# A fused attention and two-layer mixer on one core: another written order for the jobs of its first part

## The chip, the cores and the metric

The kernel runs on one core of a Trainium2 chip. The core has five engines that run side by side, each through its own list of instructions in order: TensorE (PE, matrix products; its weight loads are shown as PEld), VectorE (DVE), ScalarE (ACT), GpSimd (POOL) and SyncE (SP), which here only issues DMA transfers. An engine waits at an instruction until the semaphores it needs are set; everything behind that instruction waits too. The metric is the device time of one execution in microseconds (us), the median of several runs.

## What is computed

Everything is float32 outside; B = 2, H = 8, S = 768, D = 64.

```python
k_sum = k.reshape(B, H, 24, 32, D).max(axis=3)
v_sum = v.reshape(B, H, 24, 32, D).mean(axis=3)
scores_l = where(|t - s| < 16, q @ k.T / 8, -1e9)
scores_s = q @ k_sum.T / 8 + log(32)
a = softmax(concat([scores_l, scores_s]))
x = a @ concat([v, v_sum])                    # heads side by side: B x 768 x 512
h = relu(x @ w_in); u, v = halves(h)
v_s = w_spatial @ layernorm(v) + b_spatial
y = (u * v_s) @ w_out
h2 = relu(y @ w_in2); c = conv3(h2, conv_w)   # along the sequence
out = (h2 * sigmoid(c)) @ w_out2
```

## The kernel before

**Attention** runs over eight pairs of heads (n = 0 to 7), each in two groups of six 64-row blocks, so 16 groups. One group is a chain over four engines: PE writes masks and scores into PSUM (`qk`, L496, L503, L509), DVE takes the row maximum (L513), ACT does six exponentials with their sums (L517), DVE adds and inverts the sums (L520, L523), POOL or DVE normalises (L526), PE transposes the first half (L530), ACT or DVE copies it out of the one PSUM tile `pt` (L552), PE transposes the second half into the same `pt`, a second copy follows, PE multiplies with the values (`pv`, L536), and ACT or DVE splits the result into a high part (L557) and a low part (L558). There are two score buffers `s` and four buffers of exponentials, so several groups are under way at once. Beside that, `keys` prepares windows of k (L424, L422, L438) and block maxima (L432); `means` prepares the block means of v, for two pairs by products on PE (L452), for the others by a DVE sum (L459) and one transposition (L462), followed by a copy (L464) and spreads (L469, L471).

**Dense products** are done in three passes on high and low parts (`mm3`, L344 to L346). The first layer's weights come as raw 64-bit words and are rebuilt by `convert` (L307 or L308, L310, L312, L314, L298, L292). PE does the first layer's products (`f1u`, `f1v`) between the groups of attention, and only dense products after about 97 us. Later come the spatial mix by a seven-product scheme, the merged weights `w_out @ w_in2`, the convolution with its gate, and the last layer, again with seven products.

**What sets the order.** Every job (some instructions that belong together) is entered with `Plan.add`, with the engines that can do it and what it reads and writes. `Plan.order` then takes two tables of the file: `ORDER`, the numbers of all 1579 jobs, two characters each, in the order in which they are written out, and `PICK`, which of two or three engines does a job that can go to several. Each engine's list is its jobs in that order. `Plan.order` also adds up durations written in the file (the first number of each entry), and where PE would stand still for 0.5 us or more by these, it writes dummy products in front of the job (`warm`, L1085):

```python
gap = t - free.get(e, 0.0)
if self.fill and gap >= 0.5:
    n = int((gap - 0.1) / 0.22)
```

So the dummies depend on the order and on the file's own durations, and the table carries none of them. SP issues the loads in the order in which their jobs stand. A load into a buffer that is used again waits for the last reader of what lay there.

Of the kernel before, what the change touches and what calls it, by code (L numbers as in the profile page):

```python
# [54 lines left out]
ORDER = (
    "AAACABADAFAgAEAiAGAjAZAaAkAhAbAHAqAcAdAeArALBYAfAMBZBbBaBcAIA3A4AsAJAlAtASAUATAVAWAuAvANBiBjAKBEA5A6A7BFCTCRCUBkAmAnAwAx"
    "AOBvAyAzA8B8CVDJCSBGBwB9DKCbAoApBlBmBnAXDLA9A0A+CcA-BADHDIBxBHBoBRCoBSA1A2BBCdByBzB0BpBqCpBCAYCeAPBdCfCgBDB+DRBrB1B2C1Be"
    "BfBgBhDSEgCqCrCsB3DwEhB-AQCDDeDfB4CEBsChBICWCtBtBuCiDTBKBLEeBJBMBTBNBOCFDgCXCYCjARB5BUCZB6BVCGCHCICJB7C2CAEnETDUDVEoDrCk"
    "CuClCmCnEfCKC3CvCwCaDhDMBPDWBQFNE0DiCxEpCyCzDXC0DYEqErDsCBDxDNDODPBWDjFMDZDaDAC5DtDQFOFPDkDlC6DbDcE1E2DmDnCCDyEUFVDdDoEs"
    "EtDpEuC7C8C9C+C-BXEiDqDBCLFiEvFjE3E4EjEkDzD0EwFvCMCNDuDvCOCPD6DCDDDED7D8D9D1D+D2EEEFD3FBCQEGE5EmDFDGFkEHEIE6D4F6F7EOEPEQ"  # L60
    "ERGmD5F8F9C4FCD-EAEBECFWEXE7FFFGEYEZEaEbGnFHFIFJFKElFXEDE8GlEcEdE9FYFLGkFZFlFaGQGRGDE+ExEJEKELESHPGSGEGFEyFmE-FAFnEzFbFz"
    "F0EMFwGtG6GdEVJwFQFRFcFdF1ENHHHIGeF2F3GfGGGgF4FeHQFSFTF5FoHJFUHRGhGiGjFpFqFrGuFDG7HSHTHKHLEWFsG8GTGUGHF+GVGIFtHMHNFuFfFg"
    "HiHjFxHkHlGJFyG9G+HOHUHXHYGvGKGwHZHVFhHmHWIhGLGMF-GxGyGAHyGBHnIDHzHaGWGXImGCH0FEGoH1HbHcGYHoHqGNGZGaGbHrHsGOGcGPHdG-JtGz"
    "JuIrItIuHtIcG0H2HeGpG1HuIdIiHfIwH3GqG2IsM-INGrJxIOJzGsHvJ3HAIPHBIIHgH4HCInHDG3NBHwG4HEG5IjIvHFIXJ6IJHhJ0IEIYIKNAJ4HGNCIQ"
    "JvIeH5IZJ1IaIbIRIkIFJ5IfIxJyIyIzJBHxJCISJDHpIgILH8I0H+KbJ2H6KBJ8IlITNNKCJEH9H-IMI5H7NDKFI6IBI1I7KDIUIAIoI8JRKcJFKGI9J7NG"
    "NJJGICKHIVKXJ9JHNII2I+I3JSIWJTJUKAKYI-JJJVJIJZJaI4J-JbNEJAJcIpJKKIJWJhKEJLJdJMNFKJNHIqLDJiJeNKLHJXNUJNKQJfIGJjJ+KKJOIHKd"
    "KhJYKRJPJgLIJQKiJmKLLJJoKjNQKSJkKeNLJnLEJpJlJrLFKfKzKlKsKmKtJsKuK0KnKgKZKaLLKMLMK9KTNPLKNMK5LGKkK7LPNOLNK-K+LTNbNRKNLQNS"
    "K6NTNWLXLRLBKvLUNXLOK8LYLZLbKONVNYLVLSNiLcLdNZLALfLgLWNdLeLaKoNeLhLiNaLlLzNcKPNfLCLoL2NpLjKpNgLmNhLpNkL3NlNjLnLkL0L4MOMB"
    "NmJqKqMPMcNnKUMHL1NrNoMQNsNwKrLrNqMINtK1MEMJMRL5MCNuKVMVMdMFNzNvLqNyPXMWKWN3PLMXMDNxK3L6KwL7N0MYN1MeMmPYMnN5K4MfPMMsN2N6"
    "MGK2N4N7LvN+PZPNPaKxN8MoKyN9OAOBMKL9MzMtLsLwN-OCPbMjMuOFPOODPdOHM0PROILxPPMLMkPSOEM7OGOJMpLtPvMqPTMlMrOMPeL+OKPfPQMvOOOL"  # L70
    "OPONOTM3L-MwMxP1P2PpM4OQOUPjMMPkPUPcOaOROWMyLyOVOSMSPlOhPqM5MgM8PVPgP3PWM1MAPmMhOcM9PrOdObM6P7LuP4MZM2MiP8PnQFOXOeM+MaP5"
    "PhPsOkMbQAQGQBPwMNOjL8QCOfOiPiMTMUOoQHQDTXQIP9OYOqOrOpTYOlPtOsQJP+OgPxTdQEP-OmOvPoOtO2PyTeOuPuQXOyP6QYOxQKQcQLQdQMOwOzQZ"
    "O4QaO9O5QeO3PzQbQSQTOnQUQfO6QNQOO-OZQgQVRFO0RAPEQWQPQhPAO7PGO+QuPFP0QQQzO8O1RKQiQjQ0Q1QpTZQvPBQqQRPHQrQsQ2PIQkQwTaQxTjTf"
    "RBRLQlQtRGRcQ3TgQyRCQmQ4TpTrRDRMRHRXRIRNRYQ5TlRZU-RhRiQ6TsQnPCRdThRER2QoTbRJRsRxTiTqRORtRPTcUwRaTkTmT2UxRQQ7RjRyReQ8TtRR"
    "RfTuRzRkR3T3UrPJRTQ9RuPKR4RSR0TnRbQ+RgRlRvR5U1RmSGSLSMT6ToQ-SBRUSfSCR1RwR6PDTvTwR7SDU2SERnSHRVRoRqRpSFU6R8SIR9R+R-UySNSJ"
# [1155 lines left out]
```

## Time and profile before

| | us |
|---|---|
| median of 3 runs | 321.06 (320.39 to 321.64) |
| the profiled execution, its time | 320.22 |
| its span, first to last instruction | 318.5 |
| PE busy in the span | 310.9 |
| DVE, ACT, POOL busy | 268.8, 236.8, 117.7 |

The profiled execution took 1.7 us more than its span, and 0.84 us less than the median of the runs. Busy time on PE has modelled ends: matrix products overlap, and the end of the last one before a wait covers some of that wait. Idle time is therefore read from the starts of two jobs that follow each other, compared with the same pair where nothing is waited for.

### The profile page before, as it was taken

Reading aid. Unit: us, or ns where it says so; the run is one execution under the profiler, and the core shown is the slowest. Engines: PE = TensorE matmul, PEld = TensorE weight load, DVE = VectorE, ACT = ScalarE, POOL = GpSimd, SP = SyncE. Lnnn points to the kernel's source line nnn. Section 1 sums busy time; section 2 is a strip of 40 time slices with the busy share of each in tenths; the row PEclk is TensorE's granted clock in tenths of the full one; section 3 lists DMA queues with packets and bytes.
Section 4 is the critical chain, followed back from the end, with each engine's and each line's share of the span. In section 5 each row is a group of like instructions: output and inputs, shape, how many; then the busy total and the mean of one; then the engine's idle time right before and its main releaser. Section 6 shows DMA issues by size and latency. Waiting matters only on the chain.

```text
span 318.5 us, 6374 instructions
## 1 busy us (share of the span) xinstructions
PE 310.9 (98%) x2376; PEld 271.6 (85%) x2376; DVE 268.8 (84%) x493; ACT 236.8 (74%) x565; POOL 117.7 (37%) x130
## 2 busy tenths in 40 slices
PE   7999999999999999999999999999999999999994
PEld 3677788888888888999998888888888899999994
DVE  5989899886578978988987787899999999989971
ACT  3999888977385735677987687998788997684721
POOL 3696853814335347254532353100110222254010
PEclk9999999999999999999999999999999999999999
DMA  7999675936453001114433334400110412154432
GB/s 215 333 284 313 180 229 197 314 81 167 160 189 134 1 2 21 45 48 141 135 110 119 114 132 132 132 2 0 25 24 3 75 25 52 25 99 105 129 139 99
DMA packets 16061, 37.64 MB, mean 118 GB/s; under 512 B 1952, under 2 KB 8480, under 8 KB 16032
## 3 DMA queue, kind: packets, MB, share of 16 engines
q1 hardware_dynamic: 13728, 34.11, 33.8%
q0 software_dynamic: 2304, 3.15, 5.8%
q8 instruction: 18, 0.29, 0.4%
q14 instruction: 11, 0.09, 0.1%
HBM read 30.96 MB, written 3.15 MB: 107 GB/s over the span
## 4 chain that ended last, share of the span: by engine, by line
PE 88%; DVE 4%; ACT 3%; POOL 2%; DMA 1%; issue 1%; SPq 0%; DVEq 0%; POOLq 0%
PE late L345 11%; PE late L346 11%; PE late L344 11%; PE mm L344 10%; PE mm L346 9%; PE mm L345 9%; PE pt L530 3%; PE xp L344 3%; PE xp L345 3%; PE xp L346 3%; PE xp L536 3%; PE pt L346 3%; PE pt L344 3%; PE pt L345 3%; PE s L509 2%; DMA a<-q_in 1%
## 5 line engine op out<-in xcount | busy, mean ns | idle before, releaser
L517 ACT ACTIVATE a<-s,a 128x120 f32<-128x120 f32 x96 | 33.3, 381 | 0.9 <-DVE a L513 0.9
L345 PE MATMUL late<-xl,a 128*128 128x512 f32 (+1 forms) x80 | 29.5, 369 | 0.0
L344 PE MATMUL late<-xh,a 128*128 128x512 f32 (+1 forms) x80 | 29.4, 367 | 0.0
L346 PE MATMUL late<-xh,a 128*128 128x512 f32 (+1 forms) x80 | 29.4, 367 | 0.0
L914 DVE SCALAR_TENSOR_TENSOR w<-v,conv_t,w 128x1534 f32<-128x1534 f32 x12 | 21.8, 1818 | 4.1 <-POOL w L908 2.1
L876 POOL DMA_DIRECT2D tmp<-w x9 | 8.4, 932 | 44.3 <-ACT tmp L875 33.0
L517 ACT ACTIVATION_READ_ACCUMULATOR a<-s,a 128x1 f32 x96 | 21.9, 228 | 0.0
L526 POOL TENSOR_TENSOR a<-a,a 128x720 f32<-128x720 f32 x14 | 19.3, 1391 | 5.6 <-DVE a L523 5.5
L292 POOL TENSOR_TENSOR w<-a,w 128x256 fp32r<-128x256 f32 (+2 forms) x13 | 14.2, 1097 | 15.1 <-PE late L345 7.9
L530 PE MATMUL pt<-ident,a 128*120 128x128 f32 x96 | 16.5, 281 | 0.8 <-DVE a L552 0.6
L345 PEld LDWEIGHTS late<-xl,a 128*128 128x128 f32 x80 | 15.0, 188 | 2.4 <-DVE xl L292 0.4
L344 PEld LDWEIGHTS late<-xh,a 128*128 128x128 f32 x80 | 15.0, 188 | 1.9
L346 PEld LDWEIGHTS late<-xh,a 128*128 128x128 f32 x80 | 15.0, 188 | 1.9
L298 ACT CAST w<-a 128x512 fp32r<-128x512 f32 (+2 forms) x17 | 10.0, 589 | 8.4 <-DVE a L314 3.5
L327 ACT ACTIVATE a<-a 128x512 uint16<-128x512 uint8 x20 | 15.7, 787 | 0.0
L330 ACT ACTIVATE a<-a 128x512 f16<-128x512 f32 x20 | 15.6, 782 | 0.0
L530 PEld LDWEIGHTS pt<-ident,a 128*120 128x120 f32 x96 | 10.8, 136 | 5.0 <-POOL a L526 1.0
L513 DVE TENSOR_REDUCE a<-s 128x6 f32<-128x720 f32 x16 | 14.2, 899 | 0.9 <-PE s L509 0.8
L298 ACT CAST xh<-tmp 128x384 fp32r<-128x384 f32 x24 | 12.1, 511 | 3.8 <-DVE tmp L878 2.0
L344 PE MATMUL mm<-w,xh 128*128 128x512 f32 x36 | 14.9, 414 | 0.0
L344 PE MATMUL mm<-xh,a 128*128 128x512 f32 (+1 forms) x40 | 14.7, 367 | 0.0
L346 PE MATMUL mm<-xh,a 128*128 128x512 f32 (+1 forms) x40 | 14.7, 367 | 0.0
(399 smaller groups left out, 1131.7 us busy)
## 6 DMA issues: line engine op xcount, KB each, us to landing
a<-w_in SPq DMA_DIRECT2D x12, 512.0 KB, 3.6
...
```

The costliest lines, as they stand in the source:

```text
L292: eng.tensor_tensor(out=lo.r(), in0=src.f(), in1=hi.f(), op=ALU.subtract)
L298: us = {"ACT": (0.2 + n / 1200, lambda: ACT.copy(hi.r(), src.f())), "POOL": (0.12 + n / 1050, lambda: POOL.tensor_copy(hi.r(), src.f()))}
L327: ACT.activation(out=c.ap.bitcast(U16).rearrange("p (n w) -> p n w", w=2)[:, :, 0], in_=byte, func=AF.Copy, scale=1.0 / 32.0, bias=-15.5 / ...
L330: ACT.mul(c.ap.bitcast(F16).rearrange("p (n w) -> p n w", w=2)[:, :, 1], word(), 2.0 ** -60)
L344: PE.matmul(ps, lhsT=lh, rhs=rh, start=first and i == 0, stop=False, **kinds)
L345: PE.matmul(ps, lhsT=lh, rhs=rl, start=False, stop=False, **kinds)
L346: PE.matmul(ps, lhsT=ll, rhs=rh, start=False, stop=last and i == n - 1, **kinds)
L513: DVE.tensor_reduce(out=st[:, 0], in_=sv, op=ALU.max, axis=AX.X, negate=True)
L517: ACT.activation(out=e[:, u, :NK], in_=sv[:, u // GA, u % GA], func=AF.Exp, bias=st[:, 0, u:u + 1], accum_out=sm[:, u, :1])
L526: eng.tensor_tensor(out=e, in0=e, in1=st[:, 1].unsqueeze(2).to_broadcast([128, GB, NK]), op=ALU.mult)
L530: PE.transpose(pt3[:NK, a], e[:, GA * h + a, :NK], ident)
L914: DVE.scalar_tensor_tensor(out=two(ct)[:, bs, to], in0=two(h)[:, bs, of], scalar=scale(k), in1=two(ct)[:, bs, to], op0=ALU.mult, op1=ALU.add)
```

## The change

Only the two tables differ. Seventeen of the rows of `ORDER` are new; the first 998 of the 1579 places hold the same job numbers in another order, the last 581 are as they were. In `PICK` the first two rows are new, so some jobs change their engine: two normalisations go from POOL to DVE (POOL 14 to 12, DVE 2 to 4); three copies out of `pt`, four casts L557 and one L424 from DVE to ACT; three spreads L469 and two copies L464 from ACT to DVE, one spread L471 from POOL to DVE; one multiplication of `convert` from ACT (L307) to POOL (L308) and, later, three of the second conversion from ACT (L332) to POOL (L333); three subtractions L292 from POOL to DVE. The order of the load jobs among themselves is the same. The dummy products follow from the order: 22 become 27, 17 instead of 13 ahead of the first scores and 10 instead of 9 after them.

```diff
 ORDER = (
-    "AAACABADAFAgAEAiAGAjAZAaAkAhAbAHAqAcAdAeArALBYAfAMBZBbBaBcAIA3A4AsAJAlAtASAUATAVAWAuAvANBiBjAKBEA5A6A7BFCTCRCUBkAmAnAwAx"
+    "ACAFAGAZAgABAjAHAEAiAkAAALAMADAbAIAaAcAdAJASBZANBaAhAqAKA3ArAeAsBYAlBbBcBEATA4AUAtAVAuBiA5AWBFAOB8BjCTBGAvCRAmCUCSCVA6Bk"
...
 PICK = (
-    "001101210000101011001110100010000010100011000100011010100010111010000100010001010101001100011111011000011000100000000001"
+    "111001101100100010110100101001201100100101101000010101000000010000001200010000000110001110010011010100011001100000110001"
```

The first place is PE's list around the fourth group's transpositions, at 22 to 26 us before. `s` are scores, `a_0_100` the exponentials of the fourth group, `pt` and `xp` PSUM tiles, L462 the transposition of the v sums, `mm` the first dense product (`xh`, `xl` times `w`). Before:

```order
L509 MATMUL s_80<-a_0_95,a_0_252 64x120 x12
L530 MATMUL pt<-ident,a_0_100 120x128 x3
L462 MATMUL xp<-ident,a_0_86 24x128
L530 MATMUL pt<-ident,a_0_100 120x128 x3
L344 MATMUL mm_84<-xh_0_93,w_0_192 128x256
L345 MATMUL mm_84<-xl_0_94,w_0_192 128x256
L346 MATMUL mm_84<-xh_0_93,w_0_192 128x256
```

In the changed kernel, the same engine from the same scores on, up to the first of the two transpositions:

```order
L509 MATMUL s_80<-a_0_95,a_0_172 64x120 x12
L462 MATMUL xp<-ident,a_0_86 24x128
L344 MATMUL mm_84<-xh_0_93,w_0_232 128x256
L345 MATMUL mm_84<-xl_0_94,w_0_232 128x256
L346 MATMUL mm_84<-xh_0_93,w_0_232 128x256
L530 MATMUL pt<-ident,a_0_100 120x128 x3
```

and, after the next group's scores, the end of these scores and what follows them:

```order
L509 MATMUL s_81<-a_0_95,a_0_172 64x120 x12
L536 MATMUL xp<-a_0_92,a_0_497 64x64 x12
L530 MATMUL pt<-ident,a_0_100 120x128 x3
L452 MATMUL mm_85<-a_0_168,a_0_86 24x128 x6
```

Before, only L462 stood between the two transpositions of a group into the one tile `pt`; now a whole set of scores and a `pv` stand there, and the dense product comes ahead of both.

The second place is POOL's list from 6 to 17 us, with the first normalisations (L526; `a_0_91` and `a_0_96` are the exponentials of the first two groups). Before:

```order
L308 TENSOR_SCALAR a_0_156<-a_0_156 128x256
L424 TENSOR_SCALAR a_0_95<-a_0_96 128x6x96
L292 TENSOR_TENSOR w_0_192<-a_0_156,w_0_192 128x256
L424 TENSOR_SCALAR a_0_95<-a_0_96 128x6x96
L438 TENSOR_SCALAR a_0_95<-a_0_95 128x12x24
L526 TENSOR_TENSOR a_0_91<-a_0_91,a_0_90 128x720
L526 TENSOR_TENSOR a_0_96<-a_0_96,a_0_95 128x720
L438 TENSOR_SCALAR a_0_90<-a_0_90 128x12x24
L424 TENSOR_SCALAR a_0_90<-a_0_91 128x6x96
L471 TENSOR_SCALAR a_0_236<-a_0_97 24x768 x2
```

In the changed kernel, POOL in the same stretch, up to the third normalisation:

```order
L424 TENSOR_SCALAR a_0_90<-a_0_91 128x6x96
L424 TENSOR_SCALAR a_0_95<-a_0_96 128x6x96
L438 TENSOR_SCALAR a_0_95<-a_0_95 128x12x24
L308 TENSOR_SCALAR a_0_123<-a_0_123 128x256
L526 TENSOR_TENSOR a_0_91<-a_0_91,a_0_90 128x720
L424 TENSOR_SCALAR a_0_90<-a_0_91 128x6x96 x2
L438 TENSOR_SCALAR a_0_90<-a_0_90 128x12x24
L526 TENSOR_TENSOR a_0_96<-a_0_96,a_0_95 128x720
L471 TENSOR_SCALAR a_0_168<-a_0_97 24x768
L526 TENSOR_TENSOR a_0_97<-a_0_97,a_0_90 128x720
```

The preparation of the next pair's keys has moved between the first two normalisations, and the second spread L471 has left POOL ahead of the third.

## Rows read from the trace of the kernel before

**Rows 1.** The page: the span, and PE's busy time and instructions.
```profile
span 318.5 us, 6374 instructions
PE 310.9 (98%) x2376; PEld 271.6 (85%) x2376; DVE 268.8 (84%) x493; ACT 236.8 (74%) x565; POOL 117.7 (37%) x130
```

**Rows 2.** Busy time of each engine by stretch: length, then busy us (instructions) each.
```profile
core 0: us, PE busy (x) PEld busy (x) DVE busy (x) ACT busy (x) POOL busy (x), PEclk, DMA share, GB/s
8.73:24.80 16.07, 15.01 (x294) 11.26 (x294) 14.13 (x34) 15.50 (x79) 13.28 (x17) 1.00 1.01 305
24.80:46.46 21.66, 21.55 (x387) 17.62 (x386) 19.41 (x44) 19.38 (x74) 15.37 (x21) 1.00 0.81 242
46.46:280.00 233.54, 233.54 (x1456) 206.43 (x1456) 202.71 (x337) 180.54 (x365) 75.69 (x69) 1.00 0.31 91
280.00:296.00 16.00, 15.95 (x92) 15.61 (x91) 15.18 (x27) 9.61 (x24) 8.32 (x10) 1.00 0.56 115
```

**Rows 3.** Two of PE's four waits in the span: us in total, times, longest.
```profile
PE pt L530 <- DVE a L552: 0.6, 1, 0.6
PE mm L452 <- DMA a<-vwin: 0.2, 1, 0.2
```

**Rows 4.** PE in order of time: start, duration, line [idle before <-releaser].
```profile
1.04 4.37 PE L1085 MATMUL mm<-ones 128*128 128x512 bf16 x13 [1.04 <-DVE mhalf L1079]
...
6.88 0.85 PE L509 MATMUL s<-a,a 64*64 64x120 f32 x24 [1.19 <-DMA a<-q_in]
7.66 1.25 PE L1085 MATMUL mm<-ones 128*128 128x512 bf16 x5
8.84 0.23 PE L496 MATMUL s<-a,ones 64*64 64x72 bf16 x4
...
9.02 0.79 PE L509 MATMUL s<-a,a 64*64 64x120 f32 x24
9.90 1.49 PE L452 MATMUL mm<-a,a 96*24 96x128 f32 x12
...
12.50 1.49 PE L452 MATMUL mm<-a,a 96*24 96x128 f32 x12 [0.22 <-DMA a<-vwin]
13.97 0.54 PE L530 MATMUL pt<-ident,a 128*120 128x128 f32 x3
...
18.54 1.03 PE L1085 MATMUL mm<-ones 128*128 128x512 bf16 x4
19.66 0.54 PE L530 MATMUL pt<-ident,a 128*120 128x128 f32 x3
...
23.62 0.27 PE L462 MATMUL xp<-ident,a 128*24 128x128 f32 x1
24.50 0.54 PE L530 MATMUL pt<-ident,a 128*120 128x128 f32 x3 [0.61 <-DVE a L552]
...
38.27 0.27 PE L462 MATMUL xp<-ident,a 128*24 128x128 f32 x1
38.38 0.49 PE L530 MATMUL pt<-ident,a 128*120 128x128 f32 x3
```

**Rows 5.** The page's group of POOL's normalisations: busy us, mean ns | idle before, releaser.
```profile
L526 POOL TENSOR_TENSOR a<-a,a 128x720 f32<-128x720 f32 x14 | 19.3, 1391 | 5.6 <-DVE a L523 5.5
```

**Rows 6.** DVE in order of time, from 282 to 286 us.
```profile
282.28 0.42 DVE L292 TENSOR_TENSOR a<-a,a 128x256 fp32r<-128x256 f32 x1
...
283.55 2.39 DVE L292 TENSOR_TENSOR a<-a,a 128x256 fp32r<-128x256 f32 x1
```

**Rows 7.** POOL in order of time, in the same stretch.
```profile
284.59 1.06 POOL L292 TENSOR_TENSOR a<-tmp,a 128x256 fp32r<-128x256 f32 x1
```

**Rows 8.** The chain that ended last, at 293 us: start, us, what.
```profile
293.23 0.57 DVE xl L292
...
293.84 0.44 PE late L345
```

More of the change, by code (lines that the diff above doesn't have):

```diff
@@ L55 @@
 ORDER = (
-    "AAACABADAFAgAEAiAGAjAZAaAkAhAbAHAqAcAdAeArALBYAfAMBZBbBaBcAIA3A4AsAJAlAtASAUATAVAWAuAvANBiBjAKBEA5A6A7BFCTCRCUBkAmAnAwAx"
-    "AOBvAyAzA8B8CVDJCSBGBwB9DKCbAoApBlBmBnAXDLA9A0A+CcA-BADHDIBxBHBoBRCoBSA1A2BBCdByBzB0BpBqCpBCAYCeAPBdCfCgBDB+DRBrB1B2C1Be"
-    "BfBgBhDSEgCqCrCsB3DwEhB-AQCDDeDfB4CEBsChBICWCtBtBuCiDTBKBLEeBJBMBTBNBOCFDgCXCYCjARB5BUCZB6BVCGCHCICJB7C2CAEnETDUDVEoDrCk"
-    "CuClCmCnEfCKC3CvCwCaDhDMBPDWBQFNE0DiCxEpCyCzDXC0DYEqErDsCBDxDNDODPBWDjFMDZDaDAC5DtDQFOFPDkDlC6DbDcE1E2DmDnCCDyEUFVDdDoEs"
@@ L60 @@
[L60 to L71, printed above, removed]
@@ L72 @@
-    "PhPsOkMbQAQGQBPwMNOjL8QCOfOiPiMTMUOoQHQDTXQIP9OYOqOrOpTYOlPtOsQJP+OgPxTdQEP-OmOvPoOtO2PyTeOuPuQXOyP6QYOxQKQcQLQdQMOwOzQZ"
+    "ACAFAGAZAgABAjAHAEAiAkAAALAMADAbAIAaAcAdAJASBZANBaAhAqAKA3ArAeAsBYAlBbBcBEATA4AUAtAVAuBiA5AWBFAOB8BjCTBGAvCRAmCUCSCVA6Bk"
+    "AnAwA7AoAxB9BvDJBwAyAzBHBlCbA8ApBRBxA9BmCcA+BnA0DKA-A1APAXBACoBdA2B+BoC1CpBpAYBBBqCdByB-BzDLDHCqBCDRDICeBDBeBrDSCrB0AQDw"
+    "CDB1B2BIBKBfCfAfDeBgDTCsEfCEBsCgBJBhDfB3B4BtBMEeBuCWARDUEgChBLCiCXCjB5BNBODgCkCtCYCFDVB6CGEhCuCZCvB7DhCaBSBTC2EnBPCHClCw"
@@ new lines @@
+    "CADWCmEoDrBQETCxDiDXCKC3CnCBCyCIDMDjDYE0DAFMFODZCzDxEpC0DaDNDsDODPC5CCFNDkCJDlBUC7C6DbEUFvE1CLDcDdEqDmDQDnE2C8ErBVC9FPC+"
+    "CMDyDtEsDoFVFiEtDpDqFBBWE3C-DzCNEuD0EiDuCOE4C4D6EjBXDvDCEvFWD7DBCPD8D9D1EwFCE5CQE6F8FjD+FXDDF9EXDEGmFFEEDFEFDGE7EYF6D2EZ"
+    "EaD3D4EGFYD5EHFGE8D-EAEbEBFHFkEkECFZF7GDE9FIFlFJGQFmFzEIElEmEDF1E+ExFwGEEcGlEOGkE-EPEQFAEyGdGFGRFaEdFbEVFcERFKEzEJFQGGJw"
+    "EKF0FdESGSGnFRF2FLELFnF3EMGtFSENFDG6FUGfFeFoEWGHFpHHFTFqGeF4FrHIF+GuF5G7HPGgFsFfGhGvHQGTGiFgFhGjHRGwF-GxHJHSFtGIG8GUIcHT"
@@ new lines @@
+    "FuGJFxFyGKGAImFEGVGyIdGLHKGMGWHLG9GCJtGXInG+HiHUIrGYG-ItHXGBGNGZGoGaHjGbHYGOGcGzIoHVGPGpIuHMGqG0HNIeIwG1G2HkHlIsHmHAGrHZ"
+    "HBHaHbHWHCHOHyJ3JuJxJ6HzH0H1HnGsHDHcH2M-J5HdHEG3HFHGIIIJG4HeH3G5IfHfIpHoIKILISITIUHgJ0IVJ1JzNBIhIvIiIjJyIWIgNAH4KBJ4IkIl"
+    "KCIMNCKDKFJ2JvKGKHIXIYIZHqHrIaHsJ7HtIDIbIxIyIzNNI0HhH5HpHuHvNDHwINHxJJH+I5H8H9IEH-I6KbIOI1IqIBIFIPJ8KcH6IQI7IRI8JBI2JCJ9"
+    "JDI9JEI3ICJFI4JKJ-JLI+H7I-JRJMNGKEJGJNKJIAJAJZJHJIKAJaJOJhKIJSJTJUJbKXJiJPJcJVJQKKKQJWJjKRJdKLLHKSLIKdKzJ+KeJXNJJeNIJfKY"
@@ new lines @@
+    "JYJgNELDIGNFJmLJKfJoJkJnIHKhKiNHJpKjJlLEKZKsKaNKKtJrKlKmLFJsK9NQKgK+LKLLKuNLNPKkLMKnK7LGK5KMLXNMK0NULPJqNOLYLQNRLNNSK6LT"
+    "LZLUK-LOK8NTLRLbLVNWLcKvLaLSLWKTLfK3LALgNXLBNVNYLhNZLdLeLoLlLjNbLpNeKoLCNdLzNaLmLiL2L3NiLkKpLnK1NcLqNfKwK4NkKNMOKUNgKONp"
+    "MHMVMBL0KqMINhL1MJK2McMWMKMdL4MCNlNjMPKxMEMXKVNmMQKWMjKyNnKPMeNwMDNoMFNrMRNsMYNqNtMfNuMmMkLvMpMnMGNyN3NzMqNvMsMlMoNxLrML"
+    "N0KrN+N1N2MtN5N4L9MzMuL5MvMgMrPRPLPSN6N7MwPdN8PMN9OBPTM0PUOAPNOFN-M3PXPpLwOCPeMxM1LsPOMSOMODPYMMOEMyM7OIOGOHOJPPOKOOPZL6"
@@ L73 @@
+    "L+PjPkOLL7PQONOPPVM8LxOTM4OUP1OQMNPaPfMTORM2OaM5PqPbLtPWP2OSOWOVPlOhOcOdPgM6QAQBObPhPcOoM9L-PrL8MZOXOkLyOeQFMhOqP7PmLuTX"
+    "PvMaMUP3QCPiMAP4QDOjTYMiPsPwM+OpOiOrQGMbPnQHQIOlP8PtP5OfP9OsQJP+OgPxTdQEP-OYOmOvPoOtO2PyTeOuPuQXOyP6QYOxQKQcQLQdQMOwOzQZ"
     "O4QaO9O5QeO3PzQbQSQTOnQUQfO6QNQOO-OZQgQVRFO0RAPEQWQPQhPAO7PGO+QuPFP0QQQzO8O1RKQiQjQ0Q1QpTZQvPBQqQRPHQrQsQ2PIQkQwTaQxTjTf"
@@ L84 @@
 PICK = (
-    "001101210000101011001110100010000010100011000100011010100010111010000100010001010101001100011111011000011000100000000001"
-    "110000011001010101111000101010000001000000011000101111001001011001000110000011000000000001010001000000000100110010000010"
+    "111001101100100010110100101001201100100101101000010101000000010000001200010000000110001110010011010100011001100000110001"
+    "120000000011001110210001100100100000100001010000111001010000000000010001000010110010010010000111001000010000101000011000"
     "001000001000010010000000000000000000000000000000000000000000000000100000000000000000000000100000000100000010000000000100"
```

## The prediction

> **What bounds the kernel now.** I read the page first: PE is busy for 310.9 of 318.5 us [rows 1], far more than any other engine. Then busy time by stretch [rows 2]: from 46.46 to 280 us PE is busy for 233.54 of 233.54 us. Whatever PE gains or loses before 46.46 us is therefore carried to the end unless a later stage eats it, and behind 46.46 us there is nothing for a better order to win. Before it there is a little: PE stands idle for 1.06 us between 8.73 and 24.80 us and for 0.11 us up to 46.46 us [rows 2]. Next, PE's own waits [rows 3]: the largest in that stretch is 0.61 us for a copy L552 on DVE, then 0.22 us for a load of values. Last, PE in order of time [rows 4], for three things that the waits do not show: dummy products, which count as busy and do nothing; waits that the modelled end of the product before them covers; and how long a pair of jobs takes when nothing is waited for.
>
> So the question is small: at what time does PE, in the new order, reach the state that it had at 46.46 us? The useful products are the same in number and shape; only dummies are added.
>
> **The change part by part.** I go along PE's list.
>
> First scores. Four more dummies stand ahead of them. Five dummies fill 7.66 to 8.84 us, so one takes 0.236 us, and four take 0.94 us. PE waits 1.19 us there for q [rows 4]. The load sequence is the same, so q is not earlier; the dummies lie in that wait and cost nothing, with 0.25 us to spare. If q were much earlier they would cost up to 0.94 us.
>
> First product of means (L452). Ahead of it there are four dummies in place of five, so PE is 0.24 us earlier at it. It needs a load of values. Before, its scores end at 9.02 + 0.79 = 9.81 us and it starts at 9.90 us [rows 4]; when that load landed no row shows, since PE did not visibly wait for it. Bounds are 0 and 0.24 us gained. I take 0, because the second such product does wait for its load [rows 3], and loads that follow each other on a full DMA land late together.
>
> From there to the first transposition L530 (13.97 us before). Before: product of means, scores, product of means, with 0.22 us of waiting in between. Now: product of means, two dummies, scores, product of means. One product of means takes 12.50 to 13.97 us = 1.47 us, two dummies 0.47 us, a set of scores 0.9 to 1.0 us (8.84 to 9.81 us, less what of its end is modelled). 9.90 + 1.47 + 0.47 + 0.95 + 1.47 = 14.26 us, against 13.97 us [rows 4]. That loses 0.1 to 0.35 us; I take 0.25 us, near the upper end, since the sum of rows lies there. It also says that what moved on POOL at this place is worth nothing here: the first normalisation L526, which stood idle behind DVE's reciprocal before (POOL waits 5.6 us for L523 in all [rows 5]), comes earlier, but PE gets to its transposition only after the second product of means. What it may help is the second and third normalisation.
>
> The later dummies. Four in one place (18.54 to 19.66 us = 1.12 us [rows 4]) become four in three places, 0.94 us by the same price. The file puts them where its own durations see a wait, and rounds down, so a remainder of up to 0.3 us can be left at each place. I count 0, with bounds of 0.2 us gained and 0.6 us lost.
>
> The fourth group's transpositions. Before, the second one started 0.88 us after L462 (23.62 to 24.50 us), because the first half had to be copied out of the one tile `pt` by DVE first. Where nothing is waited for, the same pair takes 0.11 us (38.27 to 38.38 us) [rows 4]. Now three dense passes stand ahead, and a set of scores and a `pv` between the two halves: well over 1.5 us of useful work cover the round trip. Gain 0.77 us. If that cover were gone, for instance since the scores wait for a buffer, the 0.77 us come back.
>
> The rest of PE's idle time before 46.46 us is 1.06 + 0.11 - 0.61 - 0.22 = 0.34 us [rows 2, 3], in pieces; modelled ends hide perhaps 0.45 us more (some 0.09 us, 9.90 - 9.81, at five places). A different order does not keep these waits, but it makes others: I take half, a gain of 0.4 us, with bounds of 0 and 0.8 us.
>
> Sum: 0.25 - 0.77 - 0.4 = -0.92 us. With all bounds on the good side it is 0.1 - 0.24 - 0.2 - 0.77 - 0.8 = -1.9 us; with all on the bad side 0.35 + 0.6 - 0.77 = +0.2 us. Against the profiled execution this gives 320.22 - 0.9 = 319.3 us. That execution lay 0.84 us below the median of the runs, so against the median I forecast 321.06 - 0.9 = **320.2 us**.
>
> What moves between engines costs nothing as long as the engine that takes it has idle time. ACT gets copies and casts (net work in the first 35 us: a copy, a spread and two casts more, one multiplication less). It is idle for 0.57 us in the first stretch and 2.28 us in the second [rows 2]. Its new L424 and L307 stand before its first exponentials, where it waits anyway. DVE, idle for 1.94 and 2.25 us [rows 2], takes over two normalisations. POOL, with 2.8 and 6.3 us idle [rows 2], gives work away. Of the three ACT is the one with nothing to spare.
>
> The move of the normalisations meets a collision that the trace shows: a subtraction L292 on DVE that takes 0.42 us at 282.28 us takes 2.39 us at 283.55 us [rows 6], and ends 0.3 us after a subtraction on POOL that ran beside it (284.59 + 1.06 = 285.65 us [rows 7]). The Trainium skill (SBUF — State Buffer, "Who interferes with whom") says that a DVE instruction with two SBUF inputs contends with a GpSimd instruction that reads SBUF, and that the loser stands still until the other has ended; this trace agrees. By that rule alone two more normalisations on DVE would be two more chances to lock POOL out. The rows put the price of one collision at 2.39 - 0.42 = 1.97 us on the engine that loses. In the first stretch POOL has the idle time for it.
>
> **The rivals.** *The whole gain.* All waits of the first 46 us go and none comes: -1.6 to -1.9 us, 319.2 to 319.5 us. For it: DVE and POOL have idle time [rows 2], and POOL's third normalisation now has one spread less ahead of it. Against: ten dummies stand in the new list, so by the file's durations there are still waits, and ACT would have to work without a pause.
>
> *Nothing is gained.* ACT, with 0.57 us of idle time in 16 us, takes on more work; when its copies come as much later as PE comes earlier, PE waits for L552 at new places and the state of 46.46 us is reached when it was: 321.1 us. It decides at an ACT that is as often idle as before.
>
> *Slower: copies behind exponentials.* Half of PE's transpositions wait for a copy L552, and ACT's list has these copies behind whole sets of six exponentials all along the attention. Where a set starts late because its row maximum is late, the copy behind it is late and the next transposition, which before had its copy from DVE, waits. A replay that is 0.1 to 0.2 us too short at each handover loses that each time. With the 16 groups, waits of 0.2 us before some 12 of the 32 transpositions make 2.4 us, and with what PE wins at the fourth group 1.8 us slower: 322.9 us. It decides from about 1.6 us in all. For it: ACT is 96% busy from 8.73 to 24.80 us [rows 2]. Against: behind 25 us ACT has 2.28 us of air.
>
> *One more collision at the end.* From 280 to 296 us PE has 0.05 us of idle time [rows 2], and the chain that ended last runs over DVE there (DVE until 293.80 us, PE at 293.84 us [rows 8]). The jobs there stand as they did, but if they meet differently, one more collision of 1.97 us goes to the end in full: -0.9 + 1.97 gives 322.1 us. Fewer collisions would bring nothing, since PE hardly waits.
>
> **How the numbers follow.** Forecast, 319.7 to 320.7 us: 0.50. Whole gain, 319.2 to 319.5 us: 0.14. Nothing gained, 321.1 us: 0.12. One more collision, 322.1 us: 0.08. Copies behind exponentials, 322.9 us: 0.16. About 0.5% is what a measurement of this kernel can tell from no change, here 319.45 and 322.67 us. Only the whole gain lies below: 0.14 faster. The last case lies above: 0.16 slower. The other three make 0.70. The range from 319.2 to 322.7 us leaves out the upper half of the last case and a few hundredths below.
>
> **What would show it.** In the changed kernel's profile, PE in order of time: first scores at about 6.9 us, without a wait of more than 0.4 us before them (first term); first transposition at 14.1 to 14.3 us (third term); the fourth group's second transposition straight behind the `pv` ahead of it (fifth term); and dense products and attention of the first 46.46 us done about 0.9 us earlier. From 46 to 280 us PE busy without a gap. The forecast is wrong if PE's waits list a copy L552 or exponentials with over 1 us in all, if ACT idles as much as before with PE waiting for it, or if PE waits for DVE by more than 0.5 us between 280 and 296 us.

## The result, and the profile of the changed kernel

The changed kernel takes 325.18 us (median; 324.35 to 325.36), the kernel before 321.12 us in the same comparison: a ratio of 1.0121, 95% interval 1.0089 to 1.0154. It is 1.2% slower, 2.5 us above the upper end of the range. The profiled execution has a span of 322.6 us, 324.35 us in all.

The page of the changed kernel: the span, the busy time of the engines, and the chain of work that ended last. They answer to [rows 1].

```profile
span 322.6 us, 6412 instructions
...
PE 313.7 (97%) x2381; PEld 271.4 (84%) x2381; DVE 278.3 (86%) x496; ACT 235.5 (73%) x564; POOL 114.1 (35%) x128
...
PE 62%; DVE 17%; ACT 7%; DMA 5%; issue 3%; POOL 3%; SPq 0%; DVEq 0%; POOLq 0%
```

VectorE (DVE) is busy 9.5 us longer than before, although GpSimd (POOL) is busy only 3.6 us less. Here is the changed kernel's busy time in the four stretches of [rows 2], with the same columns.

```profile
8.73:24.80 16.07, 15.74 (x319) 11.97 (x323) 14.54 (x34) 15.31 (x78) 13.06 (x17) 1.00 1.02 321
24.80:46.46 21.66, 20.63 (x364) 16.33 (x356) 20.61 (x44) 19.63 (x74) 13.07 (x16) 1.00 0.81 263
46.46:280.00 233.54, 231.10 (x1435) 202.18 (x1435) 206.69 (x332) 175.52 (x356) 73.34 (x71) 1.00 0.28 86
280.00:296.00 16.00, 16.00 (x95) 15.97 (x94) 14.60 (x27) 9.94 (x24) 8.32 (x10) 1.00 0.50 86
```

TensorE (PE) stands idle for 0.33 us in the first stretch (1.06 before), as hoped. In the second it is 1.03 us (0.11 before), and from 46.46 to 280 us 2.44 us where there was none. TensorE's waits in the changed kernel (us in total, times, longest), beside [rows 3]:

```profile
PE late L344 <- DVE tmp L748: 1.5, 1, 1.5
...
PE pt L344 <- DVE tmp L748: 0.6, 1, 0.6
PE xp L536 <- issue: 0.3, 1, 0.3
PE xp L536 <- DVE xl L558: 0.3, 1, 0.3
PE pt L530 <- ACT a L552: 0.2, 1, 0.2
...
PE xp L536 <- DVE a L310: 0.2, 1, 0.2
```

The two large ones are for L748, VectorE's addition of a finished product out of PSUM into its sum in SBUF (an *eviction*: it makes the PSUM tile free), in the spatial stage. L552, the copy of which the prediction was most afraid, has 0.2 us.

The loss comes in two places. To see that, I give every job of TensorE the time that it usually takes in the kernel before, and ask at equal work done how much later the changed kernel is. Counted from 12.4 us (ahead of that, landings differ by a few tenths of a us from run to run):

| time in the kernel before, us | 27.7 | 46.5 | 93 | 135 | 142 | 168 | 318 |
|---|---|---|---|---|---|---|---|
| changed kernel later by, us | -0.46 | +0.67 | +1.98 | +1.52 | +3.30 | +4.47 | +4.27 |

So it is ahead at 27.7 us and loses 2.0 us up to 135 us, in the attention. (The value at 93 us lies higher because the two orders do not have the same jobs done there; at 135 us that is over.) Then it loses 1.8 us at one point near 140 us and 1.2 us up to 168 us. Behind 200 us nothing changes. The working is good to some 0.3 us.

What stands at those points? VectorE ahead of the eviction that TensorE waits for at 142 us (start, duration, line):

```profile
137.38 0.95 DVE L673 TENSOR_TENSOR v<-v,v 128x768 fp32r<-128x768 f32 x1
138.25 2.34 DVE L337 SCALAR_TENSOR_TENSOR a<-a,a 128x512 uint32<-128x512 uint32 x1
140.51 0.94 DVE L673 TENSOR_TENSOR xl<-a,xh 128x768 fp32r<-128x768 f32 x1
141.38 0.54 DVE L748 TENSOR_TENSOR tmp<-late,sp 128x384 f32<-128x384 f32 x1
```

GpSimd and TensorE at the same time:

```profile
137.54 2.50 POOL L680 TENSOR_TENSOR a<-a 128x768 f32<-128x768 f32 x1 [4.86 <-DVE xl L673]
...
142.07 0.41 PE L344 MATMUL late<-w,xh 128*128 128x384 f32 x1 [1.53 <-DVE tmp L748]
```

L337 (the *mask*, below: a shift and a bitwise OR that rebuild a block of weights) takes 0.68 us elsewhere. Here it began inside GpSimd's sum, which ended at 137.54 + 2.50 = 140.04 us, and the mask ended at 140.59 us. I call such an instruction *stretched*. The eviction's own product had been done at 135.9 us. The attention shows the same thing at 33 us, VectorE first, then GpSimd and TensorE:

```profile
32.86 1.61 DVE L314 SCALAR_TENSOR_TENSOR a<-a,a 128x256 uint32<-128x256 uint32 x1
34.39 0.89 DVE L513 TENSOR_REDUCE a<-s 128x6 f32<-128x720 f32 x1
35.21 0.17 DVE L523 RECIPROCAL a<-a 128x6 f32<-128x6 f32 x1
35.31 0.51 DVE L558 TENSOR_TENSOR xl<-xp,xh 128x384 fp32r<-128x384 f32 x1
...
32.66 1.52 POOL L526 TENSOR_TENSOR a<-a,a 128x720 f32<-128x720 f32 x1
...
35.87 0.51 PE L536 MATMUL xp<-a,a 120*64 120x64 f32 x10 [0.26 <-DVE xl L558]
```

L314, 0.42 us long elsewhere, lasts until 34.47 us, 0.3 us behind the end of the normalisation (34.18 us). The low part L558 that TensorE needs stands behind it.

Over the whole span VectorE's jobs that stayed on VectorE take 9.7 us more than before. Those that came to it take 23.8 us, those that left it had taken 22.0 us. So it is not the moved work that fills VectorE. Stretched time (an instruction's duration less the shortest that the same instruction has in any run, summed) is 2.4 us between 25 and 100 us before, with two instructions over 0.25 us; in the changed kernel it is 8.2 us, with eleven. From 120 to 200 us it is 2.3 us with two, and 7.0 us with seven.

That gave two theories. **S**: VectorE's stretched instructions make it late. **O**: the new order is late by itself, whatever the instructions take.

### The profile page after: what moved, and what is told of

Same layout as the page of the kernel before. It is cut to its first block, busy times and chain, and to the rows that moved or that the text cites. A ratio compares the mean times of both kernels' runs of the same rounds, so it can differ in the third digit from the quotient of the medians.

```text
span 322.6 us, 6412 instructions
## 1 busy us (share of the span) xinstructions
PE 313.7 (97%) x2381; PEld 271.4 (84%) x2381; DVE 278.3 (86%) x496; ACT 235.5 (73%) x564; POOL 114.1 (35%) x128
## 4 chain that ended last, share of the span: by engine, by line
PE 62%; DVE 17%; ACT 7%; DMA 5%; issue 3%; POOL 3%; SPq 0%; DVEq 0%; POOLq 0%
PE late L345 8%; PE late L344 8%; PE late L346 8%; PE mm L344 6%; PE mm L346 6%; PE mm L345 6%; DMA a<-w_in 3%; PE mm L1085 2%; PE xp L346 2%; PE xp L344 2%; PE pt L344 2%; PE xp L345 2%; PE pt L346 2%; PE pt L345 2%; ACT a L517 2%
## 5 line engine op out<-in xcount | busy, mean ns | idle before, releaser
L607 POOL TENSOR_TENSOR stat<-stat,mhalf 128x1 f32<-128x1 f32 x12 | 11.2, 939 | 25.3 <-DVE stat L604 25.3
L526 POOL TENSOR_TENSOR a<-a,a 128x720 f32<-128x720 f32 x12 | 17.2, 1434 | 7.9 <-DVE a L523 7.4
L337 DVE SCALAR_TENSOR_TENSOR a<-a,a 128x512 uint32<-128x512 uint32 x20 | 15.3, 767 | 3.0 <-ACT a L332 2.2
L292 POOL TENSOR_TENSOR w<-a,w 128x256 fp32r<-128x256 f32 (+1 forms) x11 | 10.3, 942 | 14.9 <-ACT w L298 14.7
L513 DVE TENSOR_REDUCE a<-s 128x6 f32<-128x720 f32 x16 | 14.3, 901 | 1.1 <-PE s L509 1.0
L344 PE MATMUL mm<-xh,w 128*128 128x256 f32 (+1 forms) x40 | 14.7, 367 | 0.0
L344 PE MATMUL mm<-xh,a 128*128 128x512 f32 (+1 forms) x40 | 14.7, 367 | 0.0
```

What stands on the lines that cost most here:

```text
L337: add({"DVE": (0.69, lambda: DVE.scalar_tensor_tensor(out=fu.u(), in0=fu.u(), scalar=3, in1=c.u(), op0=ALU.logical_shift_left, op1=ALU.bit ...
L344: PE.matmul(ps, lhsT=lh, rhs=rh, start=first and i == 0, stop=False, **kinds)
L513: DVE.tensor_reduce(out=st[:, 0], in_=sv, op=ALU.max, axis=AX.X, negate=True)
L526: eng.tensor_tensor(out=e, in0=e, in1=st[:, 1].unsqueeze(2).to_broadcast([128, GB, NK]), op=ALU.mult)
L607: add({"POOL": (0.86, lambda: POOL.tensor_tensor(out=st[:, 9:10], in0=st[:, 8:9], in1=mhalf, op=ALU.pow))}, r + 1, [s_], [s_])
```

## The experiments

Except in g1, g2, m1 and m2, every edit is one of the two tables; the diffs say what it does to them or to an engine's list. The brackets hold a run's ratio to the kernel before and its 95% interval.

**Which part of the order loses it (e1, e2).** The list is cut at its 600th job, about 117 us.

```diff
-seq = changed
+seq = changed[:600] + [k for k in before if k not in changed[:600]]
```
```diff
-seq = changed
+seq = before[:600] + [k for k in changed if k not in before[:600]]
```

> The first 600 jobs (to about 117 us, the attention and two thirds of the channel stage) in the order and on the engines of the changed kernel, all others in the order and on the engines of the kernel before. In the changed kernel's trace TensorE is some 1.5 us behind the kernel before at equal work where this cut lies, and 4.3 us behind at 166 us. Theory T (the larger part is lost by the order of the jobs behind the cut): the second loss goes, 1.5 us stay, 322.6 us. Rival H (VectorE arrives at the cut with too much work left, so the order of the head loses it all): 325.2 us, and TensorE still waits about 1.5 us for a VectorE eviction near 142 us.

> The other half: the first 600 jobs as in the kernel before, the rest in the order and on the engines of the changed kernel. Theory T: 2.7 us lost behind 130 us and nothing ahead of it, 323.8 us, with a wait of TensorE for VectorE's eviction (line 748) near 140 us. Rival H: 321.1 us, no such wait.

e2 takes 323.39 us against 320.81 us, 1.0088 (1.0049 to 1.0126): 2.6 us, and from the cut on its trace falls 2.6 us behind. So the second half of the changed order loses 2.6 us with the old first half ahead of it. Its profiled execution (326.45 us) lost 2.9 us more ahead of the cut, where TensorE's granted clock was 0.72 from 26 to 29 us (a mean between its two levels, 2.4 and 1.2 GHz), behind idle stretches of 0.61 and 1.28 us; the median has nothing of that. e1 takes 326.23 us, 1.0144 (1.0092 to 1.0196), no less than the whole change: with the new head the old tail has waits for L748 of 1.9 and 0.9 us, and there too instructions ahead of them are stretched (L608, 0.54 us elsewhere, takes 1.52 us at 128.3 us). Neither theory's number was right for e1. A part of one list and a part of another meet in a way that neither list was made for.

**Order alone, engines alone (e3, e4).**

```diff
-PICK = changed
+PICK = before
```
```diff
-ORDER = changed
+ORDER = before
```

> The changed kernel's order with every job on the engine it has in the kernel before. If the order alone makes the loss: 325.2 us. If the 31 jobs on other engines make it (two normalisations and three copies of the next layer's scores on VectorE, additions moved between VectorE and GpSimd): 321.1 us. If both share it: 322.5 to 324.

> The order of the kernel before with every job on the engine it has in the changed kernel. If the order makes the loss: 321.1 us. If the engines make it: 325.2 us. Over 325.2 us would say that the engines were chosen for the new order and cost more without it.

340.22 us (1.0583) and 343.92 us (1.0697). 99 jobs change their engine, not the 31 that the expectation names, and each order goes badly with the other's engines. (The list in the section on the change gives the net change by kind.) The two runs tell nothing about the 4 us, only that order and engines can't be judged apart.

**One stretched instruction (f4).** The sum that stretches the mask goes from GpSimd to VectorE, at its place in the list.

```diff
-137.54 POOL L680 a<-a 128x768
+145.98 DVE  L680 a<-a 128x768
```

> The changed kernel with one job on another engine: the sum of line 680 that GpSimd runs from 137.54 to 140.04 us goes to VectorE, where it costs about 0.87 us of VectorE's list ahead of the mask of line 337. Theory S (that mask lasts 2.34 us and not 0.68 because it began inside GpSimd's sum): with GpSimd empty there it is 0.68 us again, VectorE reaches the eviction 0.8 us earlier although it has more to do, and TensorE's wait near 142 us falls from 1.70 to about 0.9 us. Rival O (the mask is long for a reason of its own, and it is only VectorE's amount of work that counts): the wait grows to about 2.6 us.

f4 takes 323.98 us in one execution. VectorE in it, at the place shown above:

```profile
138.64 0.68 DVE L337 SCALAR_TENSOR_TENSOR a<-a,a 128x512 uint32<-128x512 uint32 x1
139.24 0.95 DVE L673 TENSOR_TENSOR xl<-a,xh 128x768 fp32r<-128x768 f32 x1
140.11 0.55 DVE L748 TENSOR_TENSOR tmp<-late,sp 128x384 f32<-128x384 f32 x1
```

The mask is 0.68 us again, the eviction comes 1.27 us earlier and the wait at 142 us is gone. VectorE has more to do and is earlier: theory S for this instruction, and against O. The sum turned out to stand behind the mask in VectorE's list, at 145.98 us, and so costs its time later: a wait of 0.9 us for L748 at 148.7 us.

**Mending single places (f1, f2, f3, h1).** f1 moves two evictions ahead of the stretched instructions, f2 moves four key preparations back in the attention, f3 does both, h1 has f4's edit with the sum behind the evictions, and f1's second move.

```diff
+L748 tmp<-late,sp
 L337 a<-a,a 128x512
 L673 xl<-a,xh 128x768
-L748 tmp<-late,sp
...
+L748 tmp<-pt,tmp
 L292 w<-a,w 128x512
-L748 tmp<-pt,tmp
```
```diff
-L314 a<-a,a 128x256
 L513 a<-s
 L523 a<-a
 L558 xl<-xp,xh
+L314 a<-a,a 128x256
```

> The changed kernel with two evictions of line 748 moved forward in VectorE's list: the one that TensorE waits for at 142.07 us goes ahead of the mask of line 337 (138.25 us, 2.34 us long) and the sum of line 673, the one that it waits for at 166.71 us ahead of the low part of line 292 (164.68 us, 1.50 us long). Their own inputs from TensorE were there at 135.86 and 165.02 us. If TensorE's loss behind 130 us is VectorE arriving late at these two: both waits (1.70 and 0.81 us) go, 325.2 - 2.5 = 322.7 us. If VectorE has too much to do in this stage whatever its order: the waits move to later evictions and 325.2 us stay.

> The changed kernel with four preparations of keys (lines 310, 312, 314) moved back in VectorE's list, each behind the next thing that TensorE waits for: in the trace they began while GpSimd was in an instruction of its own and lasted 1.61, 0.93 and 0.82 us where 0.42 is usual, and TensorE then waited 0.47 us at 35.87 (line 558), 0.34 us at 42.44 (line 558) and 0.24 us at 47.08 (the total of line 458). If these stretched instructions are what TensorE is late for: 1.05 us less, 324.1 us. If the attention loses its time otherwise (ScalarE's copies and exponentials, landings): 325.2 us.

> Both edits in one, eleven words of the order apart from the changed kernel. If the losses add up: 325.2 - 2.5 - 1.05 = 321.6 us, the kernel before within 0.5 us. If time won in the attention is lost again in the spatial stage, because VectorE comes no earlier there: 322.7 us. Under 320.5 us would say that the new order is the better one once these instructions are in place.

> The changed kernel with two edits in the spatial stage alone: the sum of line 680 that GpSimd ran over the mask of line 337 goes to VectorE, behind the evictions of 150 us instead of ahead of them (its first user starts at 150 us), and the eviction that TensorE waited for at 166.71 us goes ahead of the low part of line 292. Theory S: none of the three waits near 142, 149 and 167 us is left, TensorE is behind by the attention's 1.9 us and at most 0.6 us more that it then meets near 198 us: 323.1 us. If VectorE is simply short of time in this stage: a wait of about 1 us appears elsewhere between 149 and 200 us and 324 us stay.

f1: 324.14 us (1.0092, 1.0057 to 1.0126). f2: 324.92 us (1.0116, 1.0087 to 1.0146). f3: 324.15 us (1.0100, 1.0068 to 1.0133). h1: 324.22 us (1.0089, 1.0061 to 1.0117). By the ratios (1.21% for the change, 3.9 us), f1 gives back 0.9 us, f2 0.2 us, f3 0.7 us and h1 1.0 us. All four lie within each other's intervals and overlap that of the change, so no gain is clear of noise; none reaches what was expected of it. Why, f2 shows best; here is VectorE there:

```profile
35.07 0.56 DVE L558 TENSOR_TENSOR xl<-xp,xh 128x384 fp32r<-128x384 f32 x1 [0.74 <-ACT xh L557]
35.54 1.56 DVE L314 SCALAR_TENSOR_TENSOR a<-a,a 128x256 uint32<-128x256 uint32 x1
...
38.91 0.56 DVE L558 TENSOR_TENSOR xl<-xp,xh 128x384 fp32r<-128x384 f32 x1
```

L558 is early now and its wait is gone. But L314 runs into GpSimd's next normalisation, is stretched again, to 1.56 us, and makes the next L558 late: a new wait of 0.7 us. In h1 TensorE falls behind by some 0.6, 0.3 and 0.5 us near 154, 167 and 199 us (by the working of the table) in place of the losses near 142 and 167 us; from 120 to 200 us it still has six instructions stretched by over 0.25 us, where the changed kernel has seven and the kernel before two.

**Idle time of VectorE (k1, k2).** In the changed kernel VectorE stands still for 6.2 us between 104 and 113 us. Four products of the channel stage, which could start at 88.0 us, stand at 103.7 us there. k1 moves them to 90 us, k2 has h1's edits too.

```diff
+L344 mm<-w,xh 128x512
...
 L536 pt<-a,a
...
 L344 xp<-xh,w 128x512
-L344 mm<-w,xh 128x512
```

> The changed kernel with eight jobs moved forward: the sixth block of 512 rows of the channel stage's first half, whose four products (line 593) could start at 88.0 us and stand at 103.7 us in the changed order (84.9 us in the kernel before), goes back to 90 us, with its copy (line 599), statistics (lines 602 to 604) and normalisation (lines 607, 608). In the changed kernel VectorE then stands still for 3.87, 0.45 and 1.84 us between 104 and 113 us, does 4.2 us less between 100 and 120 us than in the kernel before, and is 93% busy from 120 to 200 us. Theory W (VectorE has that work left over when TensorE needs its evictions): the idle time at 104 us goes and TensorE's waits near 142 and 167 us fall from 2.5 to under 1 us, 323 to 323.7 us. Rival: the waits come from what stands ahead of those evictions in the list and from instructions that GpSimd stretches, with the work done in time or not, as in e2 (2.0 us of waits with the block done early): 324.6 to 325.2 us.

> The same and both edits of h1_spatial_all. Theory W: with the block done early VectorE has the time that h1 lacked, the waits of 0.5 us at 154 us and 0.4 us at 199 us go too, and only the attention's 1.9 us are left: 323.0 us. Rival (other jobs of VectorE are stretched in their turn): 323.7 us or more.

k1: 325.14 us (1.0128, 1.0096 to 1.0160); k2: 324.16 us (1.0070, 1.0027 to 1.0113). In k1 VectorE's idle time falls to 4.6 us (2.9 us of it now ahead of 116 us) and the wait near 142 us to 0.9 us, and the time stays: theory W, that the block is the cause, falls. Behind 130 us k2 loses 1.4 us, h1 2.0 us, the changed kernel 2.8 us.

**All of GpSimd's reads (g1, g2, m1, m2).** The order, the engines and the dependencies between jobs stay. In g1 (changed) and g2 (before) three of GpSimd's instructions of the attention cover one block of six (the expectation says eight by mistake). In m1 and m2 its differences, sums and conversions, 52 and 51 instructions, also fill their result with zeros and read nothing. Its DMA issues, its powers of one column (L607), six scalings in the attention (L438) and a few more stay as they were.

```diff
-eng.tensor_tensor(out=e, in0=e, in1=st[:, 1].unsqueeze(2).to_broadcast([128, GB, NK]), op=ALU.mult)
+few_ = slice(0, 1 if eng is POOL else GB)
+eng.tensor_tensor(out=e[:, few_], in0=e[:, few_], in1=st[:, 1].unsqueeze(2).to_broadcast([128, GB, NK])[:, few_], op=ALU.mult)
```
```diff
+if eng is POOL:
+    return POOL.memset(lo.f(), 0.0)
 eng.tensor_tensor(out=lo.r(), in0=src.f(), in1=hi.f(), op=ALU.subtract)
```

> The changed kernel with three of GpSimd's instructions of the attention cut short: the normalisation, the scaling of the key windows and the spreading of the means cover one block of eight on GpSimd (the two latter from the third pair of heads on), the rest of the result is left out. Order, engines, dependencies and all other instructions are those of the changed kernel. Theory S (in 25 to 100 us TensorE is late because VectorE's instructions with SBUF inputs stand while GpSimd is in one; 5.1 us more of that than before, in a stretch in which VectorE is 94% busy): VectorE's busy time in 25 to 75 us falls from 47.5 to about 43 us, and TensorE is at 93 us no later than in the kernel before, where it was 1.9 us later: 325.2 - 1.9 = 323.3 us. Rival O (the order itself puts VectorE's and ScalarE's jobs too late): TensorE keeps 1.5 us or more of its lag at 93 us, 324.8 to 325.2 us.

> The control: the kernel before with the same three instructions of GpSimd cut short in the same way, which leaves out the same part of the result. TensorE never waits between 46 and 280 us in the kernel before, so both theories expect little: the round trip at 24 us may go (0.8 us), 320.0 to 320.9 us.

> The changed kernel with GpSimd's differences, sums and conversions (lines 292, 298, 308, 333, 673, 680, 716) replaced by filling their results with zeros, and its three instructions of the attention cut to one block of six: that part of the result is left out, and GpSimd reads next to nothing. Order, engines and all instructions of the other engines are those of the changed kernel. Theory S (VectorE's instructions with SBUF inputs stand while GpSimd works, 8.0 us of that between 25 and 100 us and 6.9 us between 120 and 200 us, and this is what TensorE waits for near 142 and 167 us): VectorE's stretched time falls to 1 or 2 us in either stretch, TensorE's waits behind 130 us go, and what is left is the part of the attention that g1 kept, 1.5 us: 322.6 us. Rival O (the order of VectorE's list is late by itself): 2 us or more behind 130 us stay, 324.6 us or more. If filling stretches VectorE just as much, the run tells nothing.

> The control: the kernel before with the same replaced. TensorE has no wait on VectorE there between 46 and 280 us, so both theories expect 320.3 to 321 us, less only if the waits of 280 to 296 us (lines 292 on GpSimd and VectorE) go: 1.5 us less, 319 us.

g1: 325.02 us (1.0111, 1.0076 to 1.0145), g2: 320.64 us (0.9974, 0.9946 to 1.0002). VectorE's busy time from 25 to 75 us falls from 47.5 to 44.9 us, but TensorE is still 1.5 us late at 93 us, and the two orders are 4.4 us apart, no less than without the cut: g1 by itself spoke for O. It had taken away only half of the stretched time of 25 to 100 us (8.2 to 4.1 us).

m1: **320.39 us** (0.9987, 0.9965 to 1.0010), m2: 319.32 us (0.9953, 0.9936 to 0.9969). Without nearly all of GpSimd's reads the difference between the two orders is 1.07 us instead of 4.06 us. VectorE's stretched time in m1 is 1.6 us (25 to 100 us; 1.3 in m2) and 2.1 us (120 to 200 us). VectorE in m1 where the changed kernel stalls (its lines stand 2 to 8 further down: L339 is the mask, L681 the difference L673, L756 the eviction L748):

```profile
138.82 0.69 DVE L339 SCALAR_TENSOR_TENSOR a<-a,a 128x512 uint32<-128x512 uint32 x1
139.42 0.95 DVE L681 TENSOR_TENSOR xl<-a,xh 128x768 fp32r<-128x768 f32 x1
140.29 0.55 DVE L756 TENSOR_TENSOR tmp<-late,sp 128x384 f32<-128x384 f32 x1
```

And TensorE, PEld, VectorE, ScalarE and GpSimd in m1, by stretch:

```profile
120.00:160.00 40.00, 40.00 (x218) 38.19 (x218) 37.22 (x66) 25.75 (x41) 9.86 (x16) 1.00 0.17 53
160.00:200.00 40.00, 40.00 (x193) 34.93 (x192) 34.98 (x67) 32.89 (x61) 5.08 (x12) 1.00 0.46 145
```

TensorE waits for nothing from 120 to 200 us, with VectorE in the changed order and still idle at 104 us. Behind 130 us m1 loses nothing, where the changed kernel loses 2.8 us. That settles the second loss: it is all GpSimd's. Fills are also shorter than the sums that they replace (0.74 us for 2.50), so m1 takes away GpSimd's reads and some of its time together; f4 and the lines above show the overlap itself for the instruction at 138 us.

It doesn't settle the first loss. Since m1 loses nothing behind 130 us, the 1.07 us that are left between m1 and m2 must lie in the attention, where the changed kernel had lost 1.5 us against the kernel before (table, at 135 us). So most of the attention's loss is not shown to be GpSimd's. m1's trace can't tell what it is: that execution took 322.00 us, 1.6 us over the median, with an idle stretch of 1.46 us at 46 us that nothing in the trace explains (last section).

**The gain by itself (g3, p1, p2).** g3 takes the first 150 jobs of the changed order. p1 and p2 change TensorE's list of the kernel before at one or two places.

```diff
 L530 pt<-ident,a
 L462 xp<-ident,a
-L530 pt<-ident,a
 L344 mm<-xh,w 128x256
 L345 mm<-xl,w 128x256
 L346 mm<-xh,w 128x256
+L530 pt<-ident,a
```

> The first 150 jobs (to 27.6 us) in the order and on the engines of the changed kernel, all others as in the kernel before. It holds the one gain that the changed kernel's trace shows: at 25 us its TensorE is 0.55 us ahead, since the transposition of the fourth group no longer waits 0.6 us for the copy of line 552. If that gain carries to the end: 320.3 us. If VectorE pays for it behind the cut, where the order of the kernel before expects its jobs of the first 27 us to be done elsewhere: 321 to 322 us.

> The kernel before with one product of TensorE (line 344, 128x256) moved ahead of the second transposition of the fourth group, nothing else. This is the part of the changed order on which the forecast gain of 0.77 us rested, without the moves on the other engines. If the forecast was right on the round trip and wrong only on what else the order moves: the wait of 0.61 us at 24.50 us goes, the gain carries, TensorE is 0.5 us ahead at 46 us and at the end, 320.4 us. If the vector engines behind it set the pace: the 0.5 us is lost again by 46 us in new waits, 320.9 us.

> The same, and also one set of scores (lines 496 to 509) moved ahead of a transposition at 19.66 us that waits for GpSimd's normalisation and has a run of dummies in front of it (the scores could start at 19.1 us). If gains of TensorE alone carry: 0.9 to 1.0 us, 319.9 to 320.0 us, the first version under the kernel before. If ScalarE's and VectorE's list then come late: 320.5 to 321 us.

g3: 321.99 us (1.0025, 1.0002 to 1.0048). It gains 0.45 us by 27.7 us and loses 1.6 us by 35.5 us. VectorE, GpSimd and TensorE there:

```profile
30.96 1.61 DVE L312 SCALAR_TENSOR_TENSOR a<-a,a 128x256 uint32<-128x256 uint32 x1
...
34.86 0.55 DVE L558 TENSOR_TENSOR xl<-xp,xh 128x384 fp32r<-128x384 f32 x1
...
30.85 1.43 POOL L526 TENSOR_TENSOR a<-a,a 128x720 f32<-128x720 f32 x1
...
35.46 0.92 PE L536 MATMUL xp<-a,a 120*64 120x64 f32 x24 [0.96 <-DVE xl L558]
```

Again a key preparation that began 0.11 us inside a normalisation. p1: 320.64 us (0.9992, 0.9959 to 1.0025), p2: 320.62 us (0.9984, 0.9959 to 1.0009): no difference that can be measured. In p1 the wait for L552 falls from 0.61 to 0.26 us, and the next scores then wait 0.3 us for exponentials; 0.2 us is what its trace keeps up to 64 us, where a set of scores that takes 0.79 us in the kernel before lasts 1.12 us, for no reason that the trace shows. No version here is shown to beat the kernel before.

## Why the prediction was wrong, step by step

- **The steps along TensorE's list held.** First scores at 6.78 to 6.96 us (6.9 forecast), with 0.04 us of waiting at most. The first transposition starts at 13.93 us, not 14.26: the 0.25 us to lose weren't lost, since the first product of means, which I took to wait for its load until 9.90 us, starts at 9.54 us. TensorE in the changed kernel at the fourth group (first scores and transposition ahead of it):

```profile
6.96 0.78 PE L509 MATMUL s<-a,a 64*64 64x120 f32 x24
...
9.54 1.49 PE L452 MATMUL mm<-a,a 96*24 96x128 f32 x12
...
13.93 0.54 PE L530 MATMUL pt<-ident,a 128*120 128x128 f32 x3
...
25.38 0.92 PE L536 MATMUL xp<-a,a 120*64 120x64 f32 x24 [0.19 <-ACT a L469]
26.23 0.54 PE L530 MATMUL pt<-ident,a 128*120 128x128 f32 x3
```

  The second transposition stands straight behind its `pv`, as forecast, and TensorE is 0.46 us ahead at 27.7 us. By itself, though, the round trip was worth less than the 0.77 us that I gave it: with that edit alone (p1) ScalarE's exponentials are the next thing late, 0.2 us is left at first, and the median shows no gain.
- **"The rest of PE's idle time": -0.4 us forecast, about +1.1 us measured** (from -0.46 us at 27.7 to +0.67 us at 46.5 us). This is the first term of the wrong sign, and most of it stays open: in m1 and m2 1.07 us are left in the attention. I asked which waits the new order takes away and let it make half as many; nothing in a row of before could say which it makes.
- **"Behind 46.46 us there is nothing for a better order to win."** True, and the wrong question: 2.44 us were to be lost there. The change permutes the list to about 200 us, and I read an engine without gaps as a stretch without risk. What should have been asked is by how much VectorE's results come ahead of TensorE. From 27 to 100 us, 23 of 124 jobs of TensorE in the kernel before had their last operand less than 0.6 us ahead of their start; in the changed kernel 41 of 125, and 17 under 0.15 us (4 before).
- **"What moves between engines costs nothing as long as the engine that takes it has idle time."** This is the step that failed. The moved work did cost VectorE almost nothing (23.8 us in, 22.0 us out). Its *unmoved* work got 9.7 us longer. VectorE had 2.25 us of idle time from 24.80 to 46.46 us [rows 2], and in that stretch alone its instructions are stretched by 3.1 us (0.6 before). I priced this at nothing; without GpSimd's reads 3.0 of the 4.06 us between the orders go, and behind 130 us the loss of 2.8 us is gone.
- **The collision was seen, and counted once.** [rows 6, 7] show the mechanism. But I made it a matter of two normalisations, took GpSimd for the loser, and put the one dangerous place at 280 to 296 us. There TensorE doesn't wait at all now, with the same collision in the trace (L292 takes 2.39 us at 287.83 us). Nor is 1.97 us the price of one: in the kernel before, the line ahead of [rows 7] in GpSimd's list is

```profile
283.89 1.07 POOL L292 TENSOR_TENSOR a<-a,a 128x256 fp32r<-128x256 f32 x1
```

  so VectorE's subtraction stood through two of GpSimd's. The other 18 instructions of the changed kernel that are stretched by over 0.25 us lose 0.3 to 1.7 us each, 0.7 us on average. What had to be counted is how often the two engines meet, and who stands then. VectorE's instructions with two operands in SBUF that began inside a GpSimd instruction which reads SBUF, with 0.25 us or more of it to go: 16 before, 7 of them stretched by 0.1 us or more, while in the other 9 it was GpSimd's instruction that lasted longer; 23 in the changed kernel, 22 stretched. The rival had the mechanism, with the wrong place, price and number.
- **Copies behind exponentials**, the slower rival (322.9 us), had the direction right and the cause wrong: L552 has 0.2 us of TensorE's waits.
- What is left open: the 1.07 us between m1 and m2, in the attention. In m1's trace small waits are left there, for ScalarE's spread of the means L469 (0.2 us) and the copy L552 (0.2 us). And it isn't shown why the new order meets GpSimd so much more often. By the file's own durations `Plan.order` starts no job marked `lock` on VectorE while one runs on GpSimd, or the other way round; g3's 0.11 us says how little is enough to break that on the chip. How the new table was found is not on record.

In the sixteen kernels with GpSimd's instructions whole, VectorE's instructions with two operands in SBUF (L292, L312, L314, L337, L673 and the like) began 320 times inside a GpSimd instruction that reads SBUF, with 0.25 us or more of it to go. 266 times VectorE's was stretched; the other 54 times GpSimd's instruction itself lasted over 0.15 us longer than in other runs. So one of the two stood each time. In m1 and m2 they began 13 times inside a fill, and none was stretched. The Trainium skill (SBUF — State Buffer, "Who interferes with whom") says that a VectorE instruction with two SBUF inputs contends with a GpSimd instruction that reads SBUF, not with one that only writes it; the runs agree. It also says that the order of issue decides who stands. That isn't seen in each row: the subtraction of [rows 6] began at 283.55 us, ahead of both of GpSimd's (283.89 and 284.59 us), and stood for both. And in the kernel before GpSimd's L333, begun at 185.69 us, lasted 4.43 us instead of 0.65 while seven VectorE instructions that began after it ran at their usual length.
